# Attention in front of two expert layers: keys and queries laid out with dimensions on the partitions

## The chip, the core and the metric

One core of a Trainium2 chip. TensorE (PE; its weight loads are PEld) multiplies matrices into PSUM, VectorE (DVE), ScalarE (ACT) and GpSimd (POOL) do the rest of the arithmetic, SyncE (SP) issues most DMAs. The metric is the device time of one execution in microseconds; lower is better.

## What is computed

```python
scores = q @ k^T / sqrt(64)                     # 4 sequences of 576 tokens, 8 heads of 64
scores = where(0 <= i - j < 128, scores - slope_h * |i - j|, -1e9)
attn   = exp(scores - max); attn /= sum + 1e-9
x      = attn @ v                               # 2304 tokens x 512
# experts: each token goes to the 2 best of 8 by noisy logits, weighted by their softmax
logits = x @ w_gate + log1p(exp(x @ w_noise)) * noise
out    = sum over its 2 experts e of  w_e * relu(x @ w1[e]) @ w2[e]      # 512 -> 1024 -> 512
# a gated layer on all tokens
xn     = out / rms(out) * rms_g
result = (silu(xn @ w_gate2) * (xn @ w_val)) @ w_out                     # 512 -> 1536 -> 512
```

All of it in float32. The kernel keeps that accuracy by splitting most operands into a float16 high part and a float16 low part and adding the products.

## The kernel before

Tokens come in 18 tiles of 128 (`NT`). Attention is one loop over `n` (lines 611 to 679) with four steps to a tile, each step a pair of heads, 72 steps; `n` runs ahead and behind, so that one iteration issues the scores of step n + 2, the exponentials of n + 1, the transposes of n and the values of n - 2. A query tile sees its own keys and those of the tile before; tiles 0 and 9 begin a pair of sequences and see only their own. The instructions of every engine run in the order in which the program issues them (`manual_schedule`, line 236); from n = 76 a scheduler of the framework orders them (line 614) until line 754.

A tile's way: `load_qkv` (line 249) loads raw rows of keys and queries, tokens on the partitions, `load_v` the values. `split_kq` (262) makes float16 high and low parts side by side, the high on ScalarE, the low on GpSimd. `transpose_kq` (276) is a DMA transpose that SyncE issues, which puts a head's 64 high and 64 low dimensions on 128 partitions; `swap_q` (280) copies the queries with halves exchanged. For tiles 0 and 1 `turn_kq` (313) does both on TensorE, by transposes into 128 and into 64 output columns. `scores` (330) then has two matmuls of 128 rows to a head: high x high + low x low, and low x high + high x low. `shift` (346) adds the bias on VectorE and takes the row maximum, `exps` (358) is ScalarE's exponential, `turn` (366, matmuls of line 371) transposes the probabilities in float32, `high` (373) brings them from PSUM. `values` (388): three of four steps (`WHOLE`) multiply by v in float32 (line 398); in the fourth, `low` (380) and `split_v` (269) make low parts on VectorE and three float16 matmuls to a product follow (402 to 405). `divide` (410) divides by the sum; `split_x` (423) makes the high and low part of x, `put_x` (430) turns them by a DMA transpose, or on TensorE for the last three tiles.

Routing runs inside the loop: `logits` (496) two tiles behind, `route` (505) for batches of tiles in several small parts, one an iteration (`advance`), then `scatter` (479), an indirect DMA of GpSimd that writes the rows of x to the places of their experts. `take` (569) lets expert 0's first rows be read back when tiles 0 to 9, then 0 to 13, are routed (`EARLY`). From n = 72 the loop also issues steps of expert 0 (`exp0`): `first_steps` (176) is x @ w1 (line 187) with relu on ScalarE (192) and the low part on VectorE (193), `second_steps` (204) the product with w2 (208). Weights come through `weight_steps` (100): a load into one of four staging buffers by SyncE (110), the high part on ScalarE (128), the low part on VectorE (130). `drive` (145) issues the expert's matmuls and, whenever so many columns have gone by, one step of each side job: rows of the next expert (171), weights, and so on. PSUM has three buffers `mm0` (scores), two `mm1` (transposes), two `acc` (values, second products).

What follows, seven more experts and the gated layer (lines 766 to 1154), the change doesn't touch but for `weight_steps` and `drive`.

## Time and profile before

| | us |
|---|---|
| median of 3 runs (lowest, highest) | 1026.87 (1021.13, 1027.67) |
| the profiled execution | 1031.71 |
| its span, first to last instruction | 1030.0 |
| TensorE busy in the span | 965.4 (94%) |
| VectorE, ScalarE, GpSimd busy | 685.8, 452.9, 215.2 |
| mean granted clock of TensorE | 0.976 |

Times in the profile count from the span's first instruction. Busy time of TensorE is that of its matmuls, whose ends are modelled and which overlap; what a matmul costs in a stream is the distance between starts. An engine's idle time is put down to what released the instruction that ended it. L371 is line 371 of the kernel before. The granted clock is a share of full speed; 0.5 is the lower of two levels.

### The profile page before, as it was taken

How to read it: one execution, taken by the hardware profiler on the slowest of the kernel's cores; microseconds unless marked ns; L12 is line 12 of the kernel's file. 1: busy time of each engine (PE TensorE's matmuls, PEld its weight loads, DVE VectorE, ACT ScalarE, POOL GpSimd, SP SyncE). 2: the span in 40 equal slices, each digit the busy share in tenths (PEclk: the TensorE clock that was granted, in tenths of full speed). 3: DMA queues.
4: the chain of work that ended last, by engine and by line, in shares of the span. 5: the costliest groups of instructions: out<-in, count | busy, mean ns of one | idle time of the engine just before them, and what ended most of it. 6: DMA issues, size and time to landing. Idle time of an engine off the chain costs nothing.

```text
span 1030.0 us, 18541 instructions
## 1 busy us (share of the span) xinstructions
PE 965.4 (94%) x7184; PEld 672.3 (65%) x7184; DVE 685.8 (67%) x1584; ACT 452.9 (44%) x936; POOL 215.2 (21%) x261
## 2 busy tenths in 40 slices
PE   7898878869999999999999998889999999999997
PEld 4787777555565656565656577468658848857874
DVE  7788767533767666666666468998818936863750
ACT  6787766333445454545453244433422422341320
POOL 3446552600000000000000236652230150130000
PEclk9999998989999999999999999899999999999999
DMA  9999994783948584848582032302150151122000
GB/s 234 203 228 226 261 265 113 246 203 124 221 160 218 166 222 160 230 158 224 164 226 81 21 92 83 66 28 82 27 138 2 32 123 43 31 58 57 1 11 34
DMA packets 178560, 135.52 MB, mean 132 GB/s; under 512 B 130976, under 2 KB 148128, under 8 KB 178464
## 3 DMA queue, kind: packets, MB, share of 16 engines
q1 hardware_dynamic: 172704, 115.38, 44.3%
q0 software_dynamic: 5760, 18.88, 6.0%
q8 instruction: 58, 0.95, 0.4%
q14 instruction: 38, 0.31, 0.1%
HBM read 76.81 MB, written 26.74 MB: 101 GB/s over the span
## 4 chain that ended last, share of the span: by engine, by line
PE 70%; DMA 9%; DVE 9%; POOL 4%; issue 3%; ACT 3%; SPq 2%; ACTq 0%; DVEq 0%; POOLq 0%
PE mm L1045 20%; PE acc L208 19%; PE mm L187 18%; PE acc L972 11%; DMA raw<-in_qkv 3%; DVE sums L996 3%; POOL xrows L483 2%; DMA st<-in_moe_w 2%; DMA xTg<-x 1%; DMA xq<-xg 1%; DMA kqT<-kq 1%; POOL kq L267 1%; DVE ss L354 1%; SPq L901 1%; PE mm L342 1%
## 5 line engine op out<-in xcount | busy, mean ns | idle before, releaser
L187 PE MATMUL mm<-xT,w1h 128*128 128x256 f16 (+2 forms) x1088 | 167.2, 294 | 9.2 <-DVE hl L193 9.2
L187 PEld LDWEIGHTS <-w1h 128*128 128x128 f16 x1088 | 104.9, 99 | 48.6 <-issue 10.0
L193 DVE SCALAR_TENSOR_TENSOR hl<-mm,hh 128x256 f16<-128x256 f32 (+2 forms) x136 | 63.4, 469 | 104.4 <-ACT hh L192 102.6
L208 PE MATMUL acc<-w2h,hh 128*128 128x512 f16 x320 | 122.1, 382 | 0.0
L208 PE MATMUL acc<-w2l,hh 128*128 128x512 f16 x320 | 122.0, 381 | 0.0
L208 PE MATMUL acc<-w2h,hl 128*128 128x512 f16 x320 | 121.8, 381 | 0.0
L1002 POOL TENSOR_TENSOR sw<-sums,sw 128x256 f16<-128x256 f32 x36 | 28.5, 810 | 395.6 <-ACT sw L999 395.6
L208 PEld LDWEIGHTS <-hh 128*128 128x128 f16 x640 | 62.9, 98 | 72.9 <-ACT hh L192 0.6
L1045 PE MATMUL mm<-xq,sw 128*128 128x256 f16 x864 | 100.4, 273 | 1.7 <-DMA xq<-xg 1.7
L187 PE MATMUL mm<-xT,w1l 128*128 128x256 f16 (+2 forms) x544 | 92.7, 293 | 0.0
L1045 PEld LDWEIGHTS <-sw 128*128 128x128 f16 x864 | 84.4, 98 | 12.1 <-issue 2.0
L192 ACT ACTIVATE hh<-mm 128x256 f16<-128x256 f32 (+2 forms) x136 | 56.2, 418 | 80.2 <-PE mm L187 75.6
L972 PE MATMUL acc<-oh__3438,pgl 128*128 128x512 f16 (+2 forms) x228 | 84.5, 373 | 2.9 <-DVE pgl L954 2.9
L972 PE MATMUL acc<-oh__3438,pgh 128*128 128x512 f16 (+2 forms) x228 | 84.4, 372 | 0.2 <-ACT pgh L952 0.2
L972 PE MATMUL acc<-ol__3439,pgh 128*128 128x512 f16 (+2 forms) x228 | 84.3, 372 | 0.0
L972 PEld LDWEIGHTS <-pgh 128*128 128x128 f16 x456 | 44.4, 99 | 50.7 <-issue 2.2
L363 ACT ACTIVATE pr<-ss,nm 128x256 f32<-128x256 f32 (+1 forms) x144 | 63.1, 487 | 25.2 <-DVE nm L354 23.8
L187 PEld LDWEIGHTS <-w1l 128*128 128x128 f16 x544 | 52.7, 99 | 18.1
L354 DVE CUSTOM_DVE_ANT_0 ss<-mm,bias 128x256 f32<-128x256 f32 (+1 forms) x144 | 54.1, 396 | 11.4 <-PE mm L342 6.7
L371 PE MATMUL mm<-ident,pr 128*128 128x128 f32 x272 | 47.8, 293 | 14.0 <-DVE rs L416 8.8
L230 ACT ACTIVATE ys<-acc 128x512 f32<-128x512 f32 x40 | 23.7, 593 | 84.6 <-PE acc L208 68.6
L1054 DVE TENSOR_TENSOR gt<-mm,p 128x512 f32<-128x512 f32 x24 | 16.6, 690 | 60.7 <-PE mm L1045 58.6
(208 smaller groups left out, 1937.3 us busy)
## 6 DMA issues: line engine op xcount, KB each, us to landing
st<-in_moe_w SPq DMA_DIRECT2D x64, 512.0 KB, 5.0
ybuf<-ys SPq DMA_DIRECT2D x40, 256.0 KB, 2.0
raw<-in_qkv SPq DMA_DIRECT2D x17, 512.0 KB, 5.0
st<-in_moe_w_gate SPq DMA_DIRECT2D x12, 512.0 KB, 5.4
st<-in_moe_w_val SPq DMA_DIRECT2D x12, 512.0 KB, 4.9
st<-in_moe_w_out SPq DMA_DIRECT2D x12, 512.0 KB, 5.3
v<-in_qkv SPq DMA_DIRECT2D x18, 279.0 KB, 4.8
out<-ys SPq DMA_DIRECT2D x17, 256.0 KB, 2.2
```

Of the source, the lines that this page charges most:

```text
L187: nc.tensor.matmul(hp[:, :w], w1[:, c, f * P:(f + 1) * P], xT[:, xo + c, cs], start=(n == 0), stop=(n == 3 * KC - 1))
L192: nc.scalar.activation(hh[:, f, hs], hp[:, :w], AF.Relu)
L193: nc.vector.scalar_tensor_tensor(hl[:, f, hs], hp[:, :w], 0.0, hh[:, f, hs], op0=OP.max, op1=OP.subtract)
L208: nc.tensor.matmul(yp, hx[:, f, i * P:(i + 1) * P], w2[:, f, :], start=(n == 0), stop=(n == 3 * FC - 1))
L230: nc.scalar.activation(ys, yp, AF.Copy, scale=YSC)
L354: nc.vector.tensor_tensor_reduce(out=d["ss"][:, j, c0:], in0=d["sp"][:, j, c0:], in1=bias[kind][:, 2 * d["hp"] + j, c0:], scale=-1.0 / KS, ...
L363: nc.scalar.activation(d["pr"][:, j, c0:], d["ss"][:, j, c0:], AF.Exp, scale=-1.0, bias=d["nm"][:, j:j + 1])
L371: nc.tensor.transpose(pt[:, j, kk, :], d["pr"][:, j, kk * P:(kk + 1) * P], ident)
L972: nc.tensor.matmul(op[:, ds], px[:, f, cs], w[:, f, ds], start=(k == 0), stop=(k == 3 * GC - 1))
L996: nc.vector.tensor_tensor(out=o, in0=x, in1=y, op=op)
L1002: nc.gpsimd.tensor_tensor(out=here[k][1], in0=x, in1=here[k][0], op=OP.subtract)
L1045: nc.tensor.matmul(pp, w(a, pa, c), xq[:, 4 * b + 2 * pb + c, :], start=(n == 0), stop=(n == 5))
```

## The change

The host lays keys and queries out with two heads' dimensions on the partitions (`turned` in `arrange`), so that `raw` arrives as [dimensions of two heads, 4 pairs, tokens]. `split` makes high and low parts, for a tile's keys and queries apart; the transposes and copies of before are gone. `scores` runs for two steps at once: a step's heads are now all even or all odd (`heads`), the one step's dimensions lie on partitions 0 to 63 and the other's on 64 to 127, and three products of 64 rows (high x high, high x low, low x high) are issued for both in turn. All values are multiplied in float32. At the end of attention the last tile is divided, turned and routed one iteration earlier, the low parts of the last three tiles are VectorE's, the batch that begins at tile 10 has no empty iterations, expert 0's two early pieces both go through the first product before the second, weights are loaded half a step later and paced otherwise, and the program's own order holds from beginning to end.

```diff
-        for i in range(len(srcs) + 3):
-            if i < len(srcs):
-                src = srcs[i]
-                sts.append(stage.tile([P, FE], F32, name="st").rearrange("p (a d) -> p a d", a=src.shape[1]))
-                nc.sync.dma_start(sts[i], src)
...
-            k = i - 3
-            for j in range(2):
...
+        def load():
+            src = srcs[len(sts)]
+            sts.append(stage.tile([P, FE], F32, name="st").rearrange("p (a d) -> p a d", a=src.shape[1]))
+            nc.sync.dma_start(sts[-1], src)
...
+        for _ in range(3):
+            load()
+            yield
...
+        for k, j in itertools.product(range(len(srcs)), range(2)):
+            if j and len(sts) < len(srcs):
+                load()
...
                 while s[0] <= at:
-                    next(s[2], None)
+                    if next(s[2], s) is s:
+                        break
                     s[0] += s[1]
...
-        kqT = acons.tile([P, RING, 2, H, P], F16, name="kqT")
-        HS = 2 * (HP - len(WHOLE))
-        v1s = [acons.tile([P, HS, DV], F16, name=f"v1_{i}") for i in range(RING)]
-        vls = [acons.tile([P, HS, D], F16, name=f"vl_{i}") for i in range(RING)]
-        raw, v32, kq16, qT = {}, {}, {}, {}
...
+        kT = acons.tile([P, 2, HP, RING, P], F16, name="kT")
+        raw, v32, qT = {}, {}, {}
 
...
-            raw[t] = io.tile([P, 2, H, D], F32, name="raw", bufs=3)
-            kq = qkv[t * P:(t + 1) * P, :2 * DM].rearrange("p (x h d) -> p x h d", x=2, h=H)
+            raw[t] = io.tile([P, 2, HP, P], F32, name="raw", bufs=3)
...
-        def split_kq(t, xs, lo, hs=slice(0, H)):
-            if t not in kq16:
-                kq16[t] = io.tile([P, 2, H, 2, D], F16, name="kq16", bufs=3)
...
-        def split_v(t):
...
-        def transpose_kq(t):
-            nc.sync.dma_start_transpose(kqT[:, t % RING].rearrange("p x h c -> p (x h) c"),
-                                        kq16.pop(t).rearrange("p x h a d -> p (x h a d)"))
-
-        def swap_q(t):
-            kq = kqT[:, t % RING]
-            qs = qT[t] = work.tile([P, H, P], F16, name="qs")
-            nc.vector.tensor_copy(qs[:D], kq[D:, 1])
-            nc.vector.tensor_copy(qs[D:], kq[:D, 1])
+        def split(t, x, lo, gs=slice(0, HP)):
+
+            if x and t not in qT:
+                qT[t] = work.tile([P, 2, HP, P], F16, name="qT", bufs=4)
+            y = [qT[t][:, a, gs] if x else kT[:, a, gs, t % RING] for a in range(2)]
+            nc.scalar.activation(y[0], raw[t][:, x, gs], AF.Copy)
+            lo.tensor_tensor(out=y[1], in0=raw[t][:, x, gs], in1=y[0], op=OP.subtract)
 
...
-        def turn_kq(t, hp):
-            y, hs = kq16[t], slice(2 * hp, 2 * hp + 2)
-            tp = ps.tile([P, 3, 2, P], F16, name="mm1", bufs=MM[1])
...
-            split_kq(0, slice(0, 2), nc.vector, slice(i * H // 2, (i + 1) * H // 2))
+            for x in range(2):
+                split(0, x, nc.vector, slice(i * HP // 2, (i + 1) * HP // 2))
+
+        def heads(hp):
+
+            return [hp // 2 * 4 + hp % 2 + 2 * j for j in range(2)]
 
         def scores(n):
-            t, hp = divmod(n, HP)
+
+            t = n // HP
             first = t * P % S == 0
             k0 = 1 if first else 0
-            sp = ps.tile([P, 2, 2 * P], F32, name="mm0", bufs=MM[0])
             at = [(t - 1 + kk) % RING for kk in range(k0, 2)]
             chunks = ([(P, at[0], 1)] if first else [(0, at[0], 2)] if at[1] > at[0] else
                       [(0, at[0], 1), (P, at[1], 1)])
+            for i in range(2):
+                st[n + i] = dict(t=t, hp=(n + i) % HP, k0=k0, sp=ps.tile([P, 2, 2 * P], F32, name="mm0", bufs=MM[0]))
             for j in range(2):
-                h = 2 * hp + j
                 for c, sl, w in chunks:
-                    for i, qq in enumerate((kqT[:, t % RING, 1, h, :], qT[t][:, h, :])):
-                        nc.tensor.matmul(sp[:, j, c:c + w * P], qq, kqT[:, sl:sl + w, 0, h, :],
-                                         start=(i == 0), stop=(i == 1))
-            st[n] = dict(t=t, hp=hp, k0=k0, sp=sp)
+                    for m, (a, b) in enumerate(((0, 0), (0, 1), (1, 0))):
+                        for i in range(2):
+                            h = heads((n + i) % HP)[j]
+                            ds = slice(h % 2 * D, (h % 2 + 1) * D)
+                            nc.tensor.matmul(st[n + i]["sp"][:, j, c:c + w * P], qT[t][ds, a, h // 2, :],
+                                             kT[ds, b, h // 2, sl:sl + w, :], start=(m == 0), stop=(m == 2))
 
...
-                    out=d["ss"][:, j, c0:], in0=d["sp"][:, j, c0:], in1=bias[kind][:, 2 * d["hp"] + j, c0:],
+                    out=d["ss"][:, j, c0:], in0=d["sp"][:, j, c0:], in1=bias[kind][:, heads(d["hp"])[j], c0:],
...
-            whole = d["hp"] in WHOLE
-            d["ph"] = work.tile([P, 2, 2, P], F32 if whole else F16, name="pf" if whole else "ph", bufs=3 if whole else HS // 2 + 1)
...
-        def low(n):
...
+            d["ph"] = work.tile([P, 2, 2, P], F32, name="pf", bufs=3)
+            nc.scalar.activation(d["ph"][:, :, d["k0"]:, :], d["pt"][:, :, d["k0"]:, :], AF.Copy, scale=SP_ * SX)
...
-                h = 2 * hp + j
+            for j, h in enumerate(heads(hp)):
                 for kk in range(k0, 2):
-                    o = xps[t, hp // 2][:, h % 4, :]
-                    if hp in WHOLE:
-                        nc.tensor.matmul(o[:, :VN], ph[:, j, kk, :], v32[t - 1 + kk][:, h * DV:h * DV + VN],
-                                         start=(kk == k0), stop=(kk == 1))
...
+                    nc.tensor.matmul(xps[t, hp // 2][:, h % 4, :VN], ph[:, j, kk, :],
+                                     v32[t - 1 + kk][:, h * DV:h * DV + VN], start=(kk == k0), stop=(kk == 1))
...
-            lo = nc.gpsimd if t < NT - 1 else nc.vector
+            lo = nc.gpsimd if t < NT - TURNED else nc.vector
             lo.tensor_tensor(out=x16[:, 1, :], in0=x, in1=x16[:, 0, :], op=OP.subtract)
...
-            if t0 < 11:
+            if t0 < 10:
                 yield
...
         start = {
-            -1: [lambda: split_kq(1, slice(0, 1), nc.vector), lambda: split_v(0), lambda: load_qkv(3), lambda: load_v(3)],
...
-            1: [lambda: split_kq(2, slice(1, 2), nc.gpsimd), lambda: split_v(1)],
...
-            6: [lambda: swap_q(3)],
+            -2: [lambda: split(1, 0, nc.vector), lambda: split(1, 1, nc.gpsimd), lambda: load_qkv(3), lambda: load_v(3)],
         }
...
-        exp0 = itertools.chain(*(expert_steps(0, cs) for cs in EARLY.values()))
+        exp0 = expert_steps(0, *EARLY.values())
...
-        n = -3
+        n = -2
         while n < NS + HP + 2 or routing or ending or taking:
             t, p = divmod(n, HP)
-            if n == 76:
-                order.close()
-            if n + 3 < 2 * HP:
...
-            if 0 <= n + 2 < NS:
+            if 0 <= n + 2 < NS and n % 2 == 0:
                 scores(n + 2)
             if 0 <= n < NS:
...
-            if n % 2 == 0 and HP <= n < NS + HP:
+            if n % 2 == 0 and HP <= n < NS + 2:
                 parts.append(divide((n - HP) // HP, (n - HP) // 2 % 2))
-            if 1 <= n < NS + 1:
-                low(n - 1)
+            if n == NS + 1:
+                parts.append(divide(NT - 1, 1))
             for _ in itertools.zip_longest(*parts):
...
                 next(exp0, None)
                 advance(routing)
                 advance(ending)
-                for _ in range(1 if n < 77 else 2):
-                    next(exp0, None)
-
-            if 2 <= t < NT - 2 and p == 2:
-                swap_q(t + 2)
+                next(exp0, None)
+
             if 0 <= t < NT - 4 and p == 0:
                 load_qkv(t + 4)
             if 1 <= t < NT - 3 and p == 0:
                 load_v(t + 3)
-            if 1 <= t < NT - 3:
-                if p < 2:
-                    split_kq(t + 3, slice(p, p + 1), nc.gpsimd)
-                if p == 2:
-                    transpose_kq(t + 3)
-            if 2 <= t < NT - 2 and p == 3:
-                split_v(t + 2)
+            if 0 <= t < NT - 2 and p % 2:
+                split(t + 2, p // 2, nc.gpsimd)
             for step in start.pop(n, ()):
                 step()
-            if p == (3 if NT - 6 <= t - 1 < NT - 1 else 2) and 1 <= t <= NT:
+            if p == (1 if t == NT else 3 if NT - 6 <= t - 1 < NT - 1 else 2) and 1 <= t <= NT:
                 split_x(t - 1)
             if 0 <= n < NS:
                 high(n)
 
-            if p == 3 and 1 <= t <= NT:
+            if p == (2 if t == NT else 3) and 1 <= t <= NT:
                 put_x(t - 1)
-            if n in (HP * NT + 1, HP * NT + 4) or p == 0 and 3 <= t < NT + 1:
-                r = {HP * NT + 1: NT - 2, HP * NT + 4: NT - 1}.get(n, t - 3)
+            if n in (NS + 1, NS + 3) or p == 0 and 3 <= t < NT + 1:
+                r = {NS + 1: NT - 2, NS + 3: NT - 1}.get(n, t - 3)
                 logits(r)
                 if r in batch_end:
                     (routing if r < NT - 1 else ending).append(route(*batch_end[r]))
...
             if n > 2:
                 advance(tasks)
             if p < 2 or n >= 60:
-                scatter(1 if n < 77 else 2)
-
-            for _ in range((n in (50, 53, 56, 58, 60, 62, 64, 66, 68, 70)) + (n in (72, 73) or n >= 76) * 2):
+                scatter(1 if n < 68 else 2)
+
+            if n in (50, 53, 56, 58, 60, 62, 64, 66, 68, 70, 72) or n > NS + 3:
                 next(weights0, None)
...
-    for _ in range(3):
-        next(weights1)
...
-    order.enter_context(tc.manual_schedule())
...
     drive(itertools.chain(exp0, expert_steps(0, LAST)),
-          (0, 500, row_steps(0, LAST)), (0, 3000, weights0), (0, 3000, weights1),
-          *((6000 + 6000 * i, 500, row_steps(1, cs)) for i, cs in enumerate(HALVES)),
+          (0, 0, row_steps(0, LAST)), (0, 1600, weights0), (9000, 2500, weights1),
+          *((14000 + 6000 * i, 500, row_steps(1, cs)) for i, cs in enumerate(HALVES)),
...
+    turned = [r.reshape(b * s // P, P, h // 2, 2, d).transpose(0, 3, 4, 2, 1).reshape(b * s, h // 2 * P)
+              for r in rows[:2]]
...
-    given["qkv"] = np.concatenate([r.reshape(b * s, -1) for r in rows[:2] + [v, pad]], axis=1)
+    given["qkv"] = np.concatenate([*turned, v.reshape(b * s, -1), pad], axis=1)
```

## Rows read from the trace of the kernel before

**Rows 1.** The stretches: us, busy (count) of PE, PEld, DVE, ACT, POOL, clock, DMA share, GB/s

```profile
30.00:160.00 130.00, 105.07 (x1177) 95.48 (x1175) 102.41 (x464) 94.55 (x223) 69.37 (x85) 0.94 1.11 240
...
60.00:80.00 20.00, 19.33 (x213) 17.73 (x210) 19.36 (x91) 17.64 (x43) 10.78 (x12) 1.00 1.01 234
...
178.00:249.00 71.00, 58.13 (x455) 38.48 (x453) 30.65 (x100) 23.23 (x58) 18.24 (x31) 0.90 0.70 193
...
249.00:600.00 351.00, 351.00 (x2116) 206.85 (x2115) 229.34 (x410) 161.80 (x323) 9.44 (x12) 1.00 0.60 171
```

**Rows 2.** The same view for the transposes of line 371 alone (PE, PEld)

```profile
60.00:80.00 20.00, 7.09 (x44) 4.93 (x44) 1.00 1.01 234
...
30.00:160.00 130.00, 37.21 (x217) 24.94 (x218) 0.94 1.11 240
```

**Rows 3.** Waits of TensorE, 30 to 160 us: total, times, longest

```profile
PE rt L502 <- DMA xTg<-x: 9.0, 3, 7.4
...
PE mm L371 <- DVE rs L416: 8.8, 9, 1.8
```

**Rows 4.** Timeline of SyncE's issues: start, us, engine, line, operation

```profile
92.22 1.23 SPq L434 DMA_TRANSPOSE xTg<-x  x1
...
95.25 4.47 SPq L277 DMA_TRANSPOSE kqT<-kq  x1
...
99.82 3.30 SPq L434 DMA_TRANSPOSE xTg<-x  x1
```

**Rows 5.** Timeline of TensorE's matmuls over two steps: start, us, line

```profile
63.82 0.27 PE L342 MATMUL mm<-kqT 128*128 128x256 f16 x1
...
64.26 0.60 PE L371 MATMUL mm<-ident,pr 128*128 128x128 f32 x4
...
64.70 1.03 PE L398 MATMUL acc<-v,pf 128*128 128x96 f32 x8
...
65.56 0.25 PE L502 MATMUL rt<-wgh,xTg 128*128 128x16 f16 x4
...
65.87 0.27 PE L342 MATMUL mm<-kqT 128*128 128x256 f16 x1
...
66.98 0.19 PE L402 MATMUL acc<-v,ph 128*128 128x65 f16 x1
...
67.34 0.28 PE L342 MATMUL mm<-kqT 128*128 128x256 f16 x1
```

**Rows 6.** Timeline of TensorE's weight loads at the same place

```profile
63.82 0.10 PEld L342 LDWEIGHTS <-qs 128*128 128x128 f16 x1
```

**Rows 7.** Timeline of TensorE at the start, transposes of 128 and 64 columns

```profile
5.22 0.39 PE L319 MATMUL mm<-ident,kq 128*128 128x128 f16 x2 [5.22 <-DVE kq L267]
5.54 0.32 PE L321 MATMUL mm<-ident,kq 128*64 128x128 f16 x2
5.79 0.39 PE L319 MATMUL mm<-ident,kq 128*128 128x128 f16 x2
```

**Rows 8.** The same two lines' durations: ns min/median/max

```profile
L319 PE MATMUL mm<-ident,kq x32: 219/288/314, 5.2 to 20.6; 128*128 128x128 f16 x32
...
L321 PE MATMUL mm<-ident,kq x32: 243/313/316, 5.5 to 20.7; 128*64 128x128 f16 x32
```

**Rows 9.** Groups of ScalarE, 30 to 160 us: count, busy us, mean ns, idle before

```profile
L363 ACT ACTIVATE pr<-ss,nm 128x256 f32<-128x256 f32 (+1 forms) x116 | 51.4, 492 | 20.9 <-DVE nm L354 20.3 <-DVE rs L418 0.2
...
L377 ACT ACTIVATE pf<-mm 128x512 f32<-128x512 f32 (+1 forms) x43 | 24.2, 563 | 2.0 <-PE mm L342 2.0
```

**Rows 10.** Groups of VectorE, 30 to 160 us

```profile
L283 DVE COPY qs<-kqT 64x1024 f16<-64x1024 f16 x14 | 7.6, 540 | 16.4 <-DMA kqT<-kq 16.2
```

**Rows 11.** Waits of TensorE, 178 to 249 us

```profile
PE mm L187 <- DVE hl L193: 9.2, 2, 6.8
```

**Rows 12.** The chain that ended last: start, us, what

```profile
209.24 5.74 DMA st<-in_moe_w
```

**Rows 13.** Timeline of TensorE, attention's last value matmul

```profile
178.20 0.19 PE L405 MATMUL acc<-v,pl 128*128 128x65 f16 x1
```

More of the change, by code (lines that the diff above doesn't have):

```diff
@@ L28 @@
 MM = (3, 2)
-WHOLE = (0, 1, 2)
 VN = 96
@@ L105, in weight_steps @@
         sts, last = [], None
-        for i in range(len(srcs) + 3):
-            if i < len(srcs):
-                src = srcs[i]
-                sts.append(stage.tile([P, FE], F32, name="st").rearrange("p (a d) -> p a d", a=src.shape[1]))
-                nc.sync.dma_start(sts[i], src)
-            if i < 3:
-                yield
-                continue
-            if i == 3:
-                ws += [wpool.tile([P, KC, FE], F16, name="w1h"), wpool.tile([P, KC, FE], F16, name="w1l"),
-                       wpool.tile([P, FC, DM], F16, name="w2h"), wpool.tile([P, FC, DM], F16, name="w2l")]
-            k = i - 3
-            for j in range(2):
-                fs = slice(j * n // 2, (j + 1) * n // 2)
-                if k < 4:
-                    st = sts[k][:, :, fs]
-                    hi, lo = (w[:, :, k * n + fs.start:k * n + fs.stop] for w in ws[:2])
-                else:
-                    st = sts[k][:, j:j + 1]
-                    hi, lo = (w[:, (k - 4) * m + j:(k - 4) * m + j + 1] for w in ws[2:])
-                scale = SW1 if k < 4 else SW2
-                nc.scalar.activation(hi, st, AF.Copy, scale=scale)
-                if last:
-                    nc.vector.scalar_tensor_tensor(*last, op0=OP.mult, op1=OP.subtract)
-                last = lo, st, scale, hi
-                yield
@@ new lines, in load @@
+        def load():
[5 more added lines that the diff above has]
+            yield
+        ws += [wpool.tile([P, KC, FE], F16, name="w1h"), wpool.tile([P, KC, FE], F16, name="w1l"),
+               wpool.tile([P, FC, DM], F16, name="w2h"), wpool.tile([P, FC, DM], F16, name="w2l")]
+        for k, j in itertools.product(range(len(srcs)), range(2)):
+            if j and len(sts) < len(srcs):
+                load()
+            fs = slice(j * n // 2, (j + 1) * n // 2)
+            if k < 4:
+                st = sts[k][:, :, fs]
+                hi, lo = (w[:, :, k * n + fs.start:k * n + fs.stop] for w in ws[:2])
+            else:
+                st = sts[k][:, j:j + 1]
+                hi, lo = (w[:, (k - 4) * m + j:(k - 4) * m + j + 1] for w in ws[2:])
+            scale = SW1 if k < 4 else SW2
+            nc.scalar.activation(hi, st, AF.Copy, scale=scale)
+            if last:
+                nc.vector.scalar_tensor_tensor(*last, op0=OP.mult, op1=OP.subtract)
+            last = lo, st, scale, hi
+            yield
@@ L242, in attention_moe_swiglu @@
         RING = 5
[L243 to L247 removed]
+        kT = acons.tile([P, 2, HP, RING, P], F16, name="kT")
+        raw, v32, qT = {}, {}, {}
         def load_qkv(t):
[L250 to L251 removed]
+            raw[t] = io.tile([P, 2, HP, P], F32, name="raw", bufs=3)
+            kq = qkv[t * P:(t + 1) * P, :2 * DM].rearrange("p (x g c) -> p x g c", x=2, g=HP)
             if t == 0:
[L253 to L254 removed]
+                for gs in (slice(0, HP // 2), slice(HP // 2, HP)):
+                    nc.sync.dma_start(raw[t][:, :, gs], kq[:, :, gs])
             else:
@@ L374, in high @@
             d = st[n]
-            whole = d["hp"] in WHOLE
-            d["ph"] = work.tile([P, 2, 2, P], F32 if whole else F16, name="pf" if whole else "ph", bufs=3 if whole else HS // 2 + 1)
-            nc.scalar.activation(d["ph"][:, :, d["k0"]:, :], d["pt"][:, :, d["k0"]:, :], AF.Copy,
-                                 scale=SP_ * SX if whole else SP_)
-        def low(n):
-            d = st[n]
-            pt, ph = (d[x][:, :, d["k0"]:, :].rearrange("p j k q -> p j (k q)") for x in ("pt", "ph"))
-            if d["hp"] not in WHOLE:
-                d["pl"] = work.tile([P, 2, 2, P], F16, name="pl", bufs=HS // 2 + 1)
-                pl = d["pl"][:, :, d["k0"]:, :].rearrange("p j k q -> p j (k q)")
-                nc.vector.scalar_tensor_tensor(pl, pt, SP_, ph, op0=OP.mult, op1=OP.subtract)
+            d["ph"] = work.tile([P, 2, 2, P], F32, name="pf", bufs=3)
+            nc.scalar.activation(d["ph"][:, :, d["k0"]:, :], d["pt"][:, :, d["k0"]:, :], AF.Copy, scale=SP_ * SX)
         def values(n):
```

40 lines of the change are left out of this document (2 added, 38 removed).

## The prediction

> **What bounds the kernel now.** I read the busy table by stretch first [rows 1], then the count of transposed probabilities in the same stretches [rows 2], then who TensorE waited for [rows 3], SyncE's issues [rows 4], one piece of TensorE's own timeline [rows 5 to 8], and last two groups of the other engines and what ends the attention stage [rows 9 to 13]. The reader is to see three stretches. From about 249 us on TensorE is busy without a gap (351.00 of 351.00 us) [rows 1], and the change does nothing to the work there: I price it at nothing. Up to about 178 us runs attention, whose last value matmul starts at 178.20 [rows 13]. Between 178 and 249 us the routing ends and expert 0 begins; TensorE is busy for 58.13 of those 71 us at a granted clock of 0.90 [rows 1].
>
> In attention a step (two heads of a tile of 128 tokens) has four L371 transposes, so their count gives the pace: 217 in the 130 us from 30 to 160, which is 54 steps at 2.40 us; 44 in the 20 us from 60 to 80, 11 steps at 1.82 us [rows 2]. What does a step need on TensorE? Read it from the starts in [rows 5]: four score matmuls 63.82 to 64.26, 0.44 us; four transposes to 64.70, 0.44; eight f32 value instructions to 65.56, 0.86; once a tile, logits to 65.87, 0.31; and the f16 value step, one in four, 66.98 to 67.34, 0.36. A tile is 1.76 + 1.76 + 3 x 0.86 + 0.36 + 0.31 = 6.77 us, a step 1.69. So the dense stretch runs near TensorE's own pace, with VectorE also full (19.36 of 20 us) [rows 1], and the average is 0.7 us a step slower. The reason is on SyncE and the DMA queues: DMA share is 1.11 over those 130 us [rows 1]; a tile's turns on SyncE start at 92.22 and 99.82, 7.6 us apart, of which issuing the key/query transpose alone is 4.47 [rows 4]; VectorE's swap of the turned queries waited 16.2 us for that transpose to land, the largest part of its 16.4 us idle [rows 10], and TensorE waited 9.0 us for the x transpose queued behind it on the same queue [rows 3]. The DMA transposes of keys and queries are thus what sets the pace.
>
> **The change part by part.**
> *Queries and keys arrive turned.* Sixteen DMA transposes go from SyncE (tiles 0 and 1 were turned by TensorE, eight transposes a step, which go too), with the two swap copies of each tile on VectorE and the landing they wait for [rows 10]. What is left on SyncE per tile is one load of raw, one of v and one x transpose, the last 1.23 us [rows 4]. Bytes per tile by the tile sizes: 512 + 279 KB loaded, 256 KB x transposed, 256 KB scattered, 1.33 MB; at the 240 GB/s of the stretch [rows 1] 5.6 us, under the 7.6 us found below, so DMA is hidden, with a margin of two microseconds a tile if transfers bunch. The splits into high and low keep their number and size. What is late next is TensorE itself.
>
> *Scores.* A pair of steps had 8 matmuls of 128 rows (0.88 us). It gets 12 of 64 rows, alternating between the halves of the array. If the halves run side by side these are 6 slots of 0.11 = 0.66; if not, 12 x 0.11 = 1.32. The nearest rows are the start-up transposes into 64 columns: two of them together take 0.32 us, hardly more than one (median 0.313), where two whole ones take 0.39 and one has 0.288 [rows 7, 8]. So two halves of the array do run together (halves by columns; no row shows halves by rows). I take 0.66. Each change between whole and half array costs something as well: in [rows 7, 8] a cycle of 2 whole and 2 half transposes takes 5.79 - 5.22 = 0.57 us, where three slots of 128 columns at the 0.10 us that the whole pair shows between starts (0.39 - 0.288) would be 0.30, so 0.27 for going there and back; bounds 0 (hidden in the queue) and 0.32 (two pipeline tails of 0.27 - 0.11 us [rows 5]). I take 0.20 a pair of steps. So a pair costs 0.86, a step 0.43 against 0.44.
>
> [...] By a full tail each way it would be 0.32 a pair instead of 0.20, 4 us over the stage. [...]
>
> *Values all in f32.* The f16 step becomes an f32 one: 0.86 in place of 0.36, 0.50 a tile, 0.13 a step more on TensorE. What it takes from VectorE (the low parts of p and v) and from ScalarE (v's high part) is cover, not path. TensorE's 8.8 us of waits for VectorE in the transposes [rows 3] I put down to the same low parts, which hold one of two buffers; they go.
>
> *Sum for attention.* A step is 0.43 + 0.44 + 0.86 + 0.08 = 1.81 us. The dense stretch shows 1.82 - 1.69 = 0.13 above such a sum; with VectorE relieved I take 0.10, so 1.91 a step, 7.6 a tile. There are 72 steps, of which 8 (tiles 0 and 9) have half the keys: 68 whole ones, 130 us. TensorE's first work now starts at 5.22 [rows 7] and needs no turning before the scores; with 3 us to fill the pipeline the stage ends at 5.2 + 3 + 130 = 138 us, against 178.2: 40 us.
>
> *The end of attention.* TensorE idles 71 - 58 = 13 us between 178 and 249 [rows 1]. 9.2 of them are expert 0's first matmuls waiting for VectorE [rows 11], and the chain behind it is a weight load that SyncE, held up by the read-back of rows ahead of it, issued only at 209.24 and that took 5.74 us [rows 12]; ScalarE's and VectorE's queues stood behind it. The change divides the last tile one iteration earlier, takes the low parts of two more tiles on VectorE, runs the last logits one iteration earlier, drops three empty iterations from the batch of tile 10 (so its eight scatters start sooner), puts both early pieces of expert 0 through their first product before the second, loads expert 1's weights only 9000 columns in, and issues a weight load where its buffer is already free. Each is worth up to its part of the 13 us plus the slower matmuls at the lower clock (0.90 granted over the stretch); together I take 12 us. Bounds: a loss of 6, if one load's 5.74 us comes to be waited for in a new place, since the scatters of the last tiles still stand ahead of expert 1's loads on SyncE, and a gain of 15. The scheduler that ordered iterations from 76 on is also off now, so the program's order holds there; its price lies within the same bounds.
>
> Scores of two steps take two of three buffers at once; both are free two iterations before, so no wait is added there. Behind a stall of that pair would stand the transposes and values of the step.
>
> *In all* 40 + 12 = 52: 1031.7 - 52 = 980 for the profiled execution. That one was 4.8 us above the median of the runs shown, so 975 on the median's scale.
>
> **Rivals** (times on the median's scale).
> *A. The halves don't overlap: the change doesn't do what it says.* Scores cost 1.32 + 0.20 a pair, 0.76 a step; a step 2.24, 68 of them 152, the stage ends at 161: 17 + 12 = 29 saved, 998. Against it stand [rows 7, 8], for it that they show columns, at start-up, only.
> *B. Slower: every switch between the halves drains.* The place is the twelve alternating matmuls; the price is the tail of each, 0.27 - 0.11 = 0.16 [rows 5], so 12 x 0.27 + 0.2 = 3.4 us a pair, 3.2 a step, 218 for the stage, which then ends at 226: 48 lost, 12 regained, 1063. It decides from 2.4 us a pair: there the stage ends at 190 and the tail's 12 us are used up. The 0.32 us of two half transposes in [rows 7] speaks against it.
> *C. ScalarE becomes the bound.* Per step two exponentials (0.49 each), one eviction (0.56), and a quarter of two splits of the size of an eviction, 0.28: 1.83 us if nothing overlaps [rows 9], next to TensorE's 1.81. It did 1.60 a step in the dense stretch (17.64 us in 11 steps) [rows 1, 2]. If the handing to and fro between them costs the difference, a step is 2.1, the stage ends at 151: 27 + 12 = 39 saved, 988.
>
> **How the numbers follow.** The forecast has 0.64, A 0.15, C 0.13, B 0.05, anything else 0.03. Low end: switches hidden and no overhead, 1.71 x 68 = 116, the stage ends at 124, with 13 in the tail 67 saved: 960. High end: A with half of the tail gain, 1004. The range 958 to 1004 leaves out B and little else. A measurement of this kernel can tell about 1% from no change; faster by over 1% means under 1016.6, which the forecast, A and C all give: 0.91. B is slower: 0.05. Within 1%: 0.04.
>
> **What would show it.** Right: no DMA transpose of keys or queries; score matmuls starting in pairs a few nanoseconds apart, pairs 0.11 us apart; 16 transposes L371 (or its line then) per 7.6 us; the last values near 138 us; DMA share under 0.9 in that stretch; TensorE idle under 6 us between the last values and expert 1. Wrong: score matmuls 0.11 apart singly (A) or 0.27 (B); TensorE idle on ScalarE's exponentials at every step (C); values ending after 150 us; a gap of over 5 us before expert 0's second product.

## The result and the profile after

The changed kernel took 1000.5 us (median of 4 runs, 999.46 to 1003.48), the kernel before 1026.73 beside it: ratio 0.9748, 95% interval 0.9723 to 0.9774. The forecast was 975, its range 958 to 1004. The profiled execution took 1003.48 with a span of 1001.8, where the forecast for it was 980.

The busy table by stretch, of the changed kernel (columns as in [rows 1]):

```profile
30.00:110.00 80.00, 79.77 (x989) 72.63 (x986) 57.56 (x320) 70.29 (x163) 50.38 (x58) 1.00 0.81 220
118.00:150.00 32.00, 27.36 (x266) 24.28 (x266) 21.34 (x88) 20.00 (x44) 16.53 (x25) 0.84 0.67 176
150.00:220.00 70.00, 57.47 (x441) 38.53 (x439) 31.49 (x99) 23.82 (x56) 10.38 (x17) 0.93 0.63 176
220.00:570.00 350.00, 350.00 (x2106) 205.78 (x2104) 228.33 (x408) 162.41 (x323) 8.23 (x11) 1.00 0.60 171
```

From 30 to 110 us TensorE is busy without a gap, where before it idled a fifth of the time, and the DMA share is 0.81 instead of 1.11 [rows 1]. In those 80 us stand 172 probability transposes (line 346 now), four to a whole step: 43 steps at 1.86 us, where before made 54 in 130 us [rows 2]. The other end of the table is as before: no gap from 220 us on. Between the two lie the stretches that didn't go as forecast, 118 to 150 and 150 to 220.

TensorE's timeline of one pair of steps in the changed kernel (start, us, line, count; line 318 the scores, 346 the transposes, 360 the values):

```profile
61.12 0.83 PE L318 MATMUL mm<-kT,qT 64*128 64x256 f16 x12
61.88 0.66 PE L346 MATMUL mm<-ident,pr 128*128 128x128 f32 x4
62.38 1.03 PE L360 MATMUL acc<-v,pf 128*128 128x96 f32 x8
63.24 0.60 PE L346 MATMUL mm<-ident,pr 128*128 128x128 f32 x4
63.68 1.03 PE L360 MATMUL acc<-v,pf 128*128 128x96 f32 x8
64.64 0.83 PE L318 MATMUL mm<-kT,qT 64*128 64x256 f16 x12
```

Twelve score matmuls take 0.76 us to the next start (61.12 to 61.88). Ahead of them stands a gap of 0.10: eight value matmuls at the 0.107 us of [rows 5] from 63.68 would end at 64.54, the scores start at 64.64. Together 0.86 us a pair, the forecast's number to the hundredth, as six slots of 0.11 and 0.20 for the change to half the array and back; run 5 below bears out the slots.

The last two tiles of the same kernel, TensorE's timeline, cut to scores, waits and the last values:

```profile
118.14 0.39 PE L318 MATMUL mm<-kT,qT 64*128 64x256 f16 x4
120.37 0.61 PE L318 MATMUL mm<-kT,qT 64*128 64x256 f16 x8 [1.84 <-POOL qT L267]
...
133.65 1.33 PE L393 MATMUL mm<-ident,x 128*128 128x128 f16 x8 [2.21 <-DVE x L381]
134.92 1.46 PE L318 MATMUL mm<-kT,qT 64*128 64x256 f16 x12
...
149.01 1.11 PE L360 MATMUL acc<-v,pf 128*128 128x96 f32 x8
```

The last values start at 149.01, where before the last of them stood at 178.20 [rows 13] and the first of that step at 177.88: 29 us. Up to 118.14 the stage was on the forecast's time: eight steps were left, 15.3 us at 1.91, and the values run two steps behind, so by that pace it would have ended near 137. Instead TensorE waits 1.84 us for GpSimd's low part of the queries, then 2.21 for VectorE; at the end of that wait the granted clock falls to 0.50, and twelve scores take 1.46 instead of 0.83. The busy table of that place, same kernel (the clock stands behind the five engines):

```profile
130.00:140.00 10.00, 7.67 (x74) 6.39 (x73) 7.81 (x40) 5.70 (x12) 0.00 (x0) 0.67 0.76 165
133.60:143.00 9.40, 9.23 (x74) 8.12 (x75) 5.63 (x27) 5.11 (x10) 2.04 (x4) 0.50 0.51 140
```

0.67 is a mean of two levels: in windows of a quarter of a microsecond the clock of this trace is 1.00 or 0.50, but for the windows in which it changes. From 133.60 to 143.00 the lower one holds throughout.

What GpSimd and VectorE did meanwhile, their timelines in the changed kernel (438 the indirect DMA of `scatter`, 267 the low part of queries or keys, 381 the high part of x):

```profile
118.17 0.96 POOL L438 DMA_INDIRECT xrows<-x,slots  x1 [0.23 <-issue]
119.16 1.16 POOL L267 TENSOR_TENSOR qT<-raw,qT 128x512 f16<-128x512 f32 x1
...
123.89 1.17 POOL L267 TENSOR_TENSOR kT<-raw,kT 128x512 f16<-128x512 f32 x1
125.00 1.16 POOL L267 TENSOR_TENSOR qT<-raw,qT 128x512 f16<-128x512 f32 x1
```

```profile
123.50 2.95 DVE L381 CAST x<-x 128x512 f16<-128x512 f32 x1
...
133.17 0.42 DVE L381 CAST x<-x 128x512 f16<-128x512 f32 x1
```

Six scatters stand in GpSimd's queue, the last at 118.17, ahead of the low part that the scores of tile 16 wait for. And while GpSimd runs two subtractions back to back (123.89 and 125.00), a cast on VectorE that takes 0.42 to 0.61 us at its other 17 places in this trace lasts 2.95; VectorE, which also has a batch's routing to do there, comes to the next tile's x late (133.17).

The way to expert 1, TensorE's timeline of the changed kernel (188 the first product):

```profile
167.03 0.38 PE L188 MATMUL mm<-xT,w1h 128*128 128x128 f16 x4 [2.13 <-DMA xT<-xrows]
...
203.37 1.01 PE L188 MATMUL mm<-xT,w1h 128*128 128x256 f16 x4 [4.75 <-DVE hl L194]
...
220.09 0.81 PE L188 MATMUL mm<-xT,w1h 128*128 128x384 f16 x4
```

The same product in the kernel before, TensorE's timeline:

```profile
248.59 0.81 PE L187 MATMUL mm<-xT,w1h 128*128 128x384 f16 x4
```

Expert 1's first product (384 columns) starts at 220.09, 71.1 us behind the last values. Before it started at 248.59, 70.4 behind. So in these two profiles the whole gain, 28.5 us, is attention's, and the new end brought nothing. The largest gap, 4.75 us, has the same chain behind it as the 6.8 of [rows 11, 12]. SyncE's queue, then ScalarE's timeline of the changed kernel (172 read-back of rows, 109 a weight load, 128 a weight's high part, 193 the eviction of the first product):

```profile
163.76 1.29 SPq L172 DMA_TRANSPOSE xT<-xrows  x1
165.15 0.52 SPq L109 DMA_DIRECT2D st<-in_moe_w  x1
174.29 2.61 SPq L172 DMA_TRANSPOSE xT<-xrows  x2
177.00 1.63 SPq L109 DMA_DIRECT2D st<-in_moe_w  x3
178.68 8.35 SPq L172 DMA_TRANSPOSE xT<-xrows  x3
```

```profile
200.62 1.15 ACT L128 ACTIVATE w2h<-st 128x512 f16<-128x512 f32 x2 [0.17 <-DMA st<-in_moe_w]
...
202.15 1.47 ACT L193 ACTIVATE hh<-mm 128x256 f16<-128x256 f32 x5
```

SyncE waits for the last scatter (165.67 to 174.29), then expert 1's loads go out between read-backs; ScalarE converts them in program order, and five evictions that TensorE needs stand behind the last conversion.

### The profile page after: what moved, and what is told of

Same layout as the page of the kernel before. It is cut to its first block, busy times and chain, and to the rows that moved or that the text cites. A ratio compares the mean times of both kernels' runs of the same rounds, so it can differ in the third digit from the quotient of the medians.

```text
span 1001.8 us, 18526 instructions
## 1 busy us (share of the span) xinstructions
PE 957.1 (96%) x7220; PEld 668.4 (67%) x7220; DVE 653.0 (65%) x1503; ACT 450.8 (45%) x920; POOL 212.4 (21%) x255
## 4 chain that ended last, share of the span: by engine, by line
PE 81%; DVE 8%; DMA 4%; SPq 2%; ACT 2%; issue 2%; POOL 1%; DVEq 0%; ACTq 0%; POOLq 0%
PE mm L978 20%; PE mm L188 19%; PE acc L209 19%; PE acc L905 11%; PE acc L360 5%; PE mm L346 3%; DVE sums L929 3%; PE mm L318 2%; DMA st<-in_moe_w 1%; SPq L172 1%; DMA xq<-xg 1%; SPq L834 1%; DMA xrows<-x,slots 1%; DMA raw<-in_qkv 1%; DVE pgl L887 1%
## 5 line engine op out<-in xcount | busy, mean ns | idle before, releaser
L360 PE MATMUL acc<-v,pf 128*128 128x96 f32 x544 | 73.1, 278 | 0.0
L360 PEld LDWEIGHTS acc<-v,pf 128*128 128x128 f32 x544 | 69.0, 198 | 0.0
```

Source lines behind the costliest of these rows:

```text
L360: nc.tensor.matmul(xps[t, hp // 2][:, h % 4, :VN], ph[:, j, kk, :], v32[t - 1 + kk][:, h * DV:h * DV + VN], start=(kk == k0), stop=(kk == 1))
```

## The experiments

The kernel before took 1026.73 us beside the change, 1028.84 beside runs 1 to 4, 1031.54 beside runs 5 to 8 and 1026.76 beside runs 9 to 12, so kernels are compared by their ratio to the kernel before, run beside them on the same chip (runs 1 to 4 together, 5 to 8 together, 9 to 12 together). Among these runs the changed kernel itself stands beside runs 9 to 12 alone; for runs 2 to 4, run 1 beside them, which differs from the change in nothing but the order of the scores, is a second measure. Line numbers are each kernel's own: a few lines more or less than in the change.

**1. The halves one after the other.**

```diff
-                    for m, (a, b) in enumerate(((0, 0), (0, 1), (1, 0))):
-                        for i in range(2):
+                    for i in range(2):
+                        for m, (a, b) in enumerate(((0, 0), (0, 1), (1, 0))):
```

> The changed kernel with the same twelve score matmuls of a pair of steps, but the six of one half of the array issued before the six of the other, so that neighbours use the same half. My theory (the halves run side by side, 0.11 us for two matmuls): a pair costs 12 slots of 0.11 instead of 6, 0.66 us more, 34 whole pairs, +22 us: about 1022 us. Rival (the starts in the trace look paired but the array does them one after the other): no change, 1000 us within 3.

Measured: 997.8 us, ratio 0.9694 (0.9644 to 0.9745). My expectation failed. (By the loops it is three matmuls of one half and three of the other, twice, not six and six.) TensorE's timeline of this kernel:

```profile
62.86 0.84 PE L318 MATMUL mm<-kT,qT 64*128 64x256 f16 x12
63.63 0.66 PE L346 MATMUL mm<-ident,pr 128*128 128x128 f32 x4
```

0.77 us to the next start, as with the halves in turn. Either the halves run side by side whatever the order, or a matmul of 64 rows is simply twice as fast. Experiment 5 tells these apart.

**2. The DMA transposes back, as load alone.** Two transposes a tile go out from SyncE as before, into a tile that nothing reads; the computation is whole.

```diff
                 split(t + 2, p // 2, nc.gpsimd)
+                if p == 3:
+                    spare_transposes(t + 2)
```

> The changed kernel with two spare DMA transposes for each of tiles 2 to 17, of the turned queries into a tile that nobody reads: together the size of the transpose that the change took away (128 x 2048 float16), issued by SyncE at the end of a tile. My theory (these transposes set the pace of attention before, through SyncE and the DMA queues): most of attention's gain of 29 us goes, +15 to +27 us, 1015 to 1027 us, with TensorE waiting for x transposes and ScalarE for raw. Rival (what set the pace was VectorE's swap copies and low parts, and the transposes were only queued beside them): +5 us or less.

Measured: 1020.07 us, ratio 0.9914 (0.9884 to 0.9945), 17 us more than the changed kernel's ratio and 22 us more than run 1 beside it. The profiled execution was the slowest of ten, 1028.03. Busy by stretch, TensorE's timeline, and its waits from 30 to 160 us (total, times, longest):

```profile
30.00:110.00 80.00, 67.66 (x789) 60.63 (x790) 45.49 (x246) 56.15 (x128) 41.42 (x47) 0.94 1.09 236
```

```profile
143.26 0.27 PE L462 MATMUL rt<-wgh,xTg 128*128 128x16 f16 x4 [7.93 <-DMA xTg<-x]
```

```profile
PE rt L462 <- DMA xTg<-x: 22.4, 8, 7.9
```

DMA share 1.09, nearly the 1.11 of [rows 1], and TensorE falls back from 79.77 to 67.66 busy us. What it waits for is the x transpose, which stands on the same queue. No computation reads the spare transposes, so it is their load that sets the pace. Whether it acts through SyncE's queue or through the DMA engines, this run doesn't separate; ScalarE, against my expectation, hardly waits for raw (3.8 us in two waits up to 222 us).

**3. The old end in the changed kernel.** All of the change outside the layout, the scores and the values is undone: weight loads and pacing, the last tiles' order, the early pieces, expert 1's loads, the scheduler. The core of it:

```diff
-        exp0 = expert_steps(0, *EARLY.values())
+        exp0 = itertools.chain(*(expert_steps(0, cs) for cs in EARLY.values()))
...
+            if n == 76:
+                order.close()
...
-            if n in (NS + 1, NS + 3) or p == 0 and 3 <= t < NT + 1:
+            if n in (NS + 1, NS + 4) or p == 0 and 3 <= t < NT + 1:
...
+    for _ in range(3):
+        next(weights1)
...
-          (0, 0, row_steps(0, LAST)), (0, 1600, weights0), (9000, 2500, weights1),
+          (0, 500, row_steps(0, LAST)), (0, 3000, weights0), (0, 3000, weights1),
```

> The changed kernel with the order of before at the end of attention: empty iterations of the batch from tile 10, the two early pieces of expert 0 one after the other, division, turning and logits of the last tile an iteration later, weight loads and their pace as before, the framework's scheduler from n = 76. My theory (both kernels take 70 us from the last value matmul to expert 1, because a weight load behind waits for scattered rows holds ScalarE and VectorE in both): 1000 us within 5. Rival (the new order does save its 12 us and the new attention loses them elsewhere, as by arriving before its data): +8 to +15 us, 1008 to 1015.

Measured: 994.21 us, ratio 0.9661 (0.961 to 0.9713). Neither: the old end is faster, by 9 us by the ratios and by 3.6 against run 1 beside it. Experiments 6 to 12 follow this.

**4. The fourth step's values back in float16.**

```diff
+                    if hp in WHOLE:
+                        nc.tensor.matmul(o[:, :VN], ph[:, j, kk, :], v32[t - 1 + kk][:, h * DV:h * DV + VN], ...
+                        continue
+                    nc.tensor.matmul(o[:, :D + 1], ph[:, j, kk, :], v1s[r][:, g, :D + 1], ...
+                    nc.tensor.matmul(o[:, :D], ph[:, j, kk, :], vls[r][:, g, :], ...
+                    nc.tensor.matmul(o[:, :D + 1], pl[:, j, kk, :], v1s[r][:, g, :D + 1], ...
```

> The changed kernel with the fourth step of a tile in float16 high and low parts again (values of two heads in eight). My theory (TensorE is the bound of attention from 10 to 118 us and an f32 step costs it 0.50 us more than an f16 one): 18 x 0.50 = 9 us less on TensorE, some of it given back, since VectorE then holds a buffer of the transposes longer: -4 to -9 us, 992 to 996. Rival (the low parts on VectorE and their hold on the two transpose buffers cost more than the matmuls save): 1000 us or more.

Measured: 1009.6 us, ratio 0.9798 (0.9737 to 0.9859), 5 us more by the ratios, whose intervals overlap; 12 us more than run 1 beside it, with no overlap (1003.86 to 1011.17 against 997.14 to 999.44). Busy by stretch, then the longest waits from 30 to 110 us:

```profile
30.00:110.00 80.00, 72.78 (x968) 65.30 (x967) 71.75 (x317) 67.03 (x163) 48.91 (x56) 0.98 0.80 215
```

```profile
ACT pr L350 <- DVE rs L404: 9.2, 7, 2.0
PE mm L358 <- DVE rs L402: 7.2, 6, 2.4
```

TensorE has 0.5 us a tile less to do, and idles 7 of 80 us: its transposes wait 7.2 us for VectorE and ScalarE's exponentials 9.2, VectorE being busy 71.75 instead of 57.56. By these waits the float32 step pays because it takes work from VectorE.

**5. All twelve scores on one half of the array.**

```diff
-                            ds = slice(h % 2 * D, (h % 2 + 1) * D)
+                            ds = slice(0, D)
```

The kernel leaves the second head's dimensions out of the scores; the count of instructions of every engine stays the same.

> Edit: all twelve score matmuls of a pair of steps read the same 64 partitions (the first head of each two), so only one half of TensorE's array is used; the second head's dimensions are left out of the scores, which become those of the first head. Theory 1, two halves run side by side as independent streams: the same twelve matmuls now stand in one line at 0.11 us each, 1.32 instead of 0.66 us a pair, 34 whole pairs, +22 us: 1023 us where before takes 1027 and the changed kernel 1001. Theory 2, a matmul of 64 rows just takes half the time of one of 128 rows, wherever it stands: no change, 998 to 1004 us, and the pair starts 0.76 us after the one before as now.

Measured: 1032.2 us, ratio 1.0006 (0.9989 to 1.0023): 26 us more than the changed kernel's ratio. TensorE's timeline:

```profile
59.93 1.48 PE L318 MATMUL mm<-kT,qT 64*128 64x256 f16 x12
61.34 0.66 PE L346 MATMUL mm<-ident,pr 128*128 128x128 f32 x4
...
64.44 1.48 PE L318 MATMUL mm<-kT,qT 64*128 64x256 f16 x12
```

1.41 us to the next start instead of 0.76: the same twelve matmuls in one line at 0.11. With the gap ahead that is 1.51, again 0.2 above the slots (1.32). Two halves do run side by side, and without that the whole change would gain nothing. The 26 us here and the 17 of run 2 don't add up to the gain: either TensorE's own step or the transposes' load can set the pace, and each run brings one of them back.

**6. Expert 1's first loads early.** This and the next two runs each take one part of the old end alone.

```diff
     weights1 = new_weights(1)
+    for _ in range(3):
+        next(weights1)
```

> Edit: the first three loads of expert 1's weights are issued before the read-back of expert 0's last rows, as in the kernel before; nothing else of the new end is undone. Theory 1, the end stays at 70 us because expert 1's loads stand behind the row read-backs on SyncE and their conversions ahead of the eviction of the first product on ScalarE: the 4.75 us gap before the 256-column first product and the slow clock behind it go, 5 to 7 us: 994 to 996 us where the changed kernel takes 1001. Theory 2, the loss lies in the merged early pieces or in the pacing of expert 0's weights: under 2 us gained, 999 to 1001 us.

Measured: 1007.5 us where before took 1031.54, ratio 0.9767 (0.9744 to 0.9789): no gain. ScalarE's, then TensorE's timeline:

```profile
194.76 0.63 ACT L128 ACTIVATE w2h<-st 128x512 f16<-128x512 f32 x1 [4.49 <-DMA st<-in_moe_w]
195.30 0.58 ACT L231 ACTIVATE ys<-acc 128x512 f32<-128x512 f32 x1
```

```profile
195.93 0.58 PE L209 MATMUL acc<-w2h,hh 128*128 128x512 f16 x1 [4.83 <-ACT ys L231]
```

The gap of 4.75 is gone and one of 4.83 is there: ScalarE now waits for a later load, with another eviction behind it. The wait moved.

The same trace says something of attention's end. TensorE's timeline, the first scores of tile 16 and the last values:

```profile
122.54 1.46 PE L318 MATMUL mm<-kT,qT 64*128 64x256 f16 x12
...
147.54 1.11 PE L360 MATMUL acc<-v,pf 128*128 128x96 f32 x8
```

TensorE came to tile 16 some 4 us later here, after waits of 2.7 us that the profile puts to nothing on the core. No wait for the queries' low part stands ahead of them, and for VectorE's cast of x TensorE then waited 0.92 us instead of 2.21. The last values start 25.0 us behind these scores, in the change 30.9 (118.14 to 149.01). One trace, and not an experiment made for it.

**7. The early pieces apart.**

```diff
-        exp0 = expert_steps(0, *EARLY.values())
+        exp0 = itertools.chain(*(expert_steps(0, cs) for cs in EARLY.values()))
```

> Edit: the two early pieces of expert 0 each go through first and second product before the next, as in the kernel before. Theory 2, the merged order leaves TensorE nothing to do while the second piece's rows come back (gaps of 2.13 and 1.40 us): 3 to 4 us gained, 997 to 998 us where the changed kernel takes 1001. Theory 1, expert 1's late loads set the end: no change, 1000 to 1002 us, or up to 1004 since the second product then wants w2 earlier.

Measured: 1010.43 us, ratio 0.9799 (0.9779 to 0.9819): slower by 3 us than run 6 beside it, and by 4 than run 8. TensorE's timeline:

```profile
196.00 0.59 PE L188 MATMUL mm<-xT,w1h 128*128 128x128 f16 x4 [8.29 <-DVE hl L194]
```

With expert 1's loads as late as in the change, the eviction of the next first product waits behind them for 8.29 us. By this trace merging the pieces hides part of those loads.

**8. The old pacing of expert 0's weights.**

```diff
-            if n in (50, 53, 56, 58, 60, 62, 64, 66, 68, 70, 72) or n > NS + 3:
+            for _ in range((n in (50, 53, 56, 58, 60, 62, 64, 66, 68, 70)) + (n in (72, 73) or n >= 76) * 2):
```

> Edit: expert 0's weights are converted two steps an iteration at the end of attention, as in the kernel before, instead of one. Theory 3, the last weight load of expert 0, which in the changed kernel stands behind a row read-back on SyncE and holds ScalarE from 165.8 to 171.6 us, goes ahead of it: 2 to 4 us gained, 997 to 999 us where the changed kernel takes 1001. Theory 1, expert 1's late loads set the end: 1000 to 1002 us.

Measured: 1006.59 us, ratio 0.9759 (0.974 to 0.9779): no change from the changed kernel's ratio.

**9 to 12. Old and new end, each with and without the scheduler,** on one chip. Run 9 is the change as it is, run 12 is run 3's kernel again; run 10 is the change with these lines, run 11 the old end without them:

```diff
+            if n == 76:
+                order.close()
...
+    order.enter_context(tc.manual_schedule())
     coming = {}
```

> The changed kernel without an edit, as the measure for the three beside it: ratio to before 0.973 to 0.977, about 1002 us where before takes 1028.

> Edit: the program from the 76th step of attention to the drive of expert 0 is ordered by the scheduler again, as in the kernel before; everything else of the new end stays. Theory 4, the hand order is what the end lost: TensorE's short waits for VectorE's counts and for ScalarE get first-product matmuls in front of them again, 4 to 9 us gained over the changed kernel beside it, ratio to before 0.966 to 0.971. Theory 5, the order of the work itself (merged pieces, expert 1's loads at 9000 columns, low parts on VectorE) is what the end lost: under 2 us from the changed kernel beside it.

> Edit: all of the new end undone except that the scheduler stays off. Theory 4, the hand order is what the end lost: no faster than the changed kernel beside it, ratio 0.973 to 0.980. Theory 5, the order of the work itself is what the end lost: as fast as the old end with the scheduler on, 5 to 9 us under the changed kernel.

> The whole old end in the changed kernel once more, now on one chip with the changed kernel: both theories expect 6 to 9 us under the changed kernel beside it, ratio 0.966 to 0.969; if it comes within 2 us of it, its first result owed to the chip and the end costs nothing either way.

Measured, before at 1026.76:

| | order by hand | scheduler |
|---|---|---|
| new end | 1000.09, 0.9741 (0.9724 to 0.9758) | 999.68, 0.9739 (0.9717 to 0.9761) |
| old end | 997.27, 0.9716 (0.9698 to 0.9734) | 993.03, 0.9674 (0.9656 to 0.9692) |

The old end with the scheduler is 7 us faster than the change beside it. The scheduler alone brings nothing, the old order alone 3 us, where the intervals overlap; both together 7. (The two profiled executions, 998.37 and 994.83, differ by half of that.) So neither theory holds as put. TensorE's timeline of the changed kernel once more, of the new end with the scheduler, and of the old end with it (runs 9, 10 and 12):

```profile
152.24 0.17 PE L494 MATMUL rt<-m,tri 128*128 128x8 f16 x1 [1.69 <-DVE m L488]
...
164.93 0.45 PE L188 MATMUL mm<-xT,w1h 128*128 128x128 f16 x4 [2.01 <-DMA xT<-xrows]
...
199.36 1.01 PE L188 MATMUL mm<-xT,w1h 128*128 128x256 f16 x4 [4.12 <-DVE hl L194]
```

```profile
155.48 0.17 PE L494 MATMUL rt<-m,tri 128*128 128x8 f16 x1 [0.17 <-DVE m L488]
...
168.08 0.54 PE L188 MATMUL mm<-xT,w1h 128*128 128x128 f16 x4 [5.00 <-DMA xT<-xrows]
...
200.63 0.60 PE L188 MATMUL mm<-xT,w1h 128*128 128x256 f16 x4 [3.31 <-DVE hl L194]
```

```profile
171.42 0.38 PE L185 MATMUL mm<-xT,w1h 128*128 128x128 f16 x4 [0.52 <-DMA xT<-xrows]
...
183.34 0.58 PE L185 MATMUL mm<-xT,w1h 128*128 128x128 f16 x4 [7.08 <-DVE hl L191]
```

The scheduler does fill the short waits for the routing's counts (1.69 becomes 0.17), by pulling first products forward; in the merged order it then runs out of them, and the wait for the second piece's rows grows from 2.01 to 5.00 us. In the old order the second product of the first piece stands there, and that wait is 0.52. The wait for expert 1's loads stays in each: 4.12, 3.31 and 7.08 us.

## Why the prediction was right and wrong

- **What bounded the kernel: right.** Put back as mere load, the transposes take back 17 of the 26 us, 22 against run 1 (run 2). How much of that is SyncE's queue and how much the DMA engines stays open.
- **Scores at 0.86 us a pair: right,** 0.66 of slots and 0.20 of switching, in the changed kernel and, with 1.32 of slots, in run 5. Rival A is out, but its price was too low: it was put at 998, and run 5 took as long as before. Its step was sized well (2.24; run 5's pair lasts 4.51); what failed with it was the same end of attention and tail as below. Rival B is out, and the halves need not even alternate (run 1).
- **Weight loads: without a term in the sum, and none was needed.** Run 1 puts three matmuls of one half in a row, and the pair takes 0.77 us against 0.76 with the halves in turn; run 5's twelve, all on one half, start 0.11 us apart, as a single half's slots were priced. Inside these pairs no wait stands in the rows of either run, and the twelve weight loads of a pair last 0.56 us in run 1 and 0.55 in the change.
- **Values in float32: right in that they take load from VectorE,** wrong in calling it cover, not path: TensorE's waits for VectorE come back in run 4, and 5 us with them by the ratios, 12 against run 1 beside it.
- **A step of 1.91 us: right** (1.86 measured). Rival C is out: ScalarE is busy 70.29 of 80 us and TensorE has no gap.
- **"The stage ends at 138": wrong by 11 us.** The step that failed is 68 steps all at the dense pace. It held until 118 us. The last eight steps, with the values behind them, took 31 us instead of 19. GpSimd and VectorE had been costed at nothing there, but their work for routing and x bunches in the last tiles, and the faster TensorE no longer leaves them room. By the change's trace the 12 us are 4.4 of waits (the two shown and one of 0.33), about 5 of the lower clock (some ten microseconds at half speed) and about 2 of work that the sum of a step doesn't hold: the first twelve matmuls of expert 0, ahead of the last values, and x turned on TensorE. The last two figures are estimates from that trace. The clock is 1.00 up to 133.25 us and 0.50 from 133.50, the second wait ends at 133.65; what made it fall is not shown. In run 6 the first of these waits is missing and the second is 0.92, though it has others and slow scores too (twelve in 1.46 us at 122.54), and the same piece took 25 us instead of 31 there. Moving the scatters or the subtractions was not tried.
- **"Together I take 12 us" for the end: wrong by 12.7.** The forecast added up what each edit might remove. The runs show that the gaps are not a sum: they are one chain (scatter lands, rows are read back, expert 1's loads go out, ScalarE converts in order, evictions behind), and each edit moves the wait to the next thing in it (runs 6 to 8). The edits of the end cost 7 us together against the old end with its scheduler (run 12; run 3 has 9 by the ratios and 3.6 against run 1). The bound of a loss of 6 "if one load's 5.74 us comes to be waited for in a new place" was nearer the truth than the value I took. Which of the old end's parts make up the 3 us without the scheduler, if they are more than noise, stays open.

11 and 12.7 make up, to a few tenths, the 23.5 us between 980 and 1003.48. That 1000.5 lies in the range all the same is partly luck: its high end, 1004, was rival A with half of the tail's gain, and nothing in it stood for the two steps that failed. Of the signs put down, the pace of a step and the DMA share (0.81) came as forecast; the last values at 138 and less than 6 us of idle ahead of expert 1 did not (149, and 12.5 from 150 to 220), and the values end just behind the 150 that was to mean wrong.

The fastest kernel here keeps the layout, scores and values of the change and the end of the kernel before: ratio 0.9674.

## What to carry to other kernels

Price a packed matmul by slots of one half plus one switch each way (here 0.11 us a slot and 0.20 for both switches). When a stage gets faster, go through the last iterations engine by engine, those too whose work was hidden before: side jobs bunch there, and the average pace says nothing of them. Gaps with one queue behind them are not added up: take away the first, and ask which instruction is waited for next before crediting the gain.

## What was not expected of the hardware

- Two half-array streams overlap though three matmuls in a row go to the same half: 0.77 us a pair in run 1, 1.41 with one half only (run 5). Six in a row, with both halves in the pair, were not tried.
- VectorE's float32 to float16 cast of 128x512 took 2.95 us in the first profile of the change, beside two subtractions of GpSimd. It starts at 123.50, 0.39 us ahead of the first subtraction, and ends at 126.45, the second subtraction at 126.16. A cast of 2.95 us stands at the same place in the second profile (run 9, 124.15) and in run 3 (122.95). The other casts took 0.42 to 0.66 in the traces before and after, those beside a scatter among them, and none of these has more than 0.11 us of a subtraction beside it. That the subtractions held it is my reading of these durations; no run took them away alone.
- The same program's granted clock from 118 us on differs between executions: 0.67 from 130 to 140 us in the first profile of the change, 0.83 in the second, with spans of 1001.8 and 996.7.
- In the traces of runs 6 to 8 ScalarE has three waits of 2.5 to 4.0 us (in runs 6 and 8 they end between 150 and 168 us) that the profile puts to nothing on the core, and TensorE has 2.6 to 2.9 us of them between 116 and 120; the change's first trace has none there, nor has TensorE in the second. Run 5, run together with them (5.3 and 3.7 us on ScalarE), and the kernel before (7.68 us on ScalarE at 203.93) have such waits too, so they don't come of the edits of runs 6 to 8 alone. Their cause stays open, and those runs were judged against each other and by their ratio.
